# A transformer of four layers on one core: the second weight matrix loaded in two parts, and a new written order of instructions

## Chip, cores and metric

The kernel runs on one core of one Trainium2 chip. The metric is the device time of one execution in microseconds (us); of the kernel before nine runs are shown, and their median counts. TensorE (PE) multiplies matrices, with weight loads (PEld) that overlap the multiplications; ScalarE (ACT), VectorE (DVE) and GpSimd (POOL) work on tiles; SyncE (SP) issues most of the DMAs, ACT a few.

## What is computed

Four layers on 2048 tokens of 512 channels, 32 heads of 16 channels, everything handed over in bf16. Layers 1 and 3 are attention with a sliding window of 256 tokens (A), layers 2 and 4 linear attention over all tokens (B). Each pair uses the same weights twice.

```python
def _A_ref(x, wqkv, wo):
    B, S, D = x.shape
    H = 32; Dh = D // H; W = 256
    qkv = (lambda x, *d: x.transpose(*d))((x @ wqkv).reshape(B, S, 3, H, Dh), 2, 0, 3, 1, 4)
    q, k, v = qkv[0], qkv[1], qkv[2]
    scores = jnp.einsum("bhqd,bhkd->bhqk", q, k) * (Dh ** -0.5)
    idx = jnp.arange(S)
    mask = (idx[:, None] - idx[None, :] >= 0) & (idx[:, None] - idx[None, :] < W)
    scores = jnp.where(mask[None, None], scores, -1e9)
    p = _softmax(scores, axis=-1)
    o = jnp.einsum("bhqk,bhkd->bhqd", p, v)
    return (lambda x, *d: x.transpose(*d))(o, 0, 2, 1, 3).reshape(B, S, D) @ wo

def _B_ref(x, wqkv, wo):
    ...
    phi = lambda t: jnp.where(t > 0, t + 1, jnp.exp(t)) + 1e-6
    pq, pk = phi(q), phi(k)
    kv = jnp.einsum("bhsd,bhse->bhde", pk, v)
    z = jnp.einsum("bhsd->bhd", pk)
    num = jnp.einsum("bhqd,bhde->bhqe", pq, kv)
    den = jnp.einsum("bhqd,bhd->bhq", pq, z)[..., None] + 1e-6
    o = num / den
    return (lambda x, *d: x.transpose(*d))(o, 0, 2, 1, 3).reshape(B, S, D) @ wo

x = A_x
x = x + _A_ref(_layernorm(x, axis=-1), A_wqkv, A_wo)
x = x + _B_ref(_layernorm(x, axis=-1), B_wqkv, B_wo)
x = x + _A_ref(_layernorm(x, axis=-1), A_wqkv, A_wo)
x = x + _B_ref(_layernorm(x, axis=-1), B_wqkv, B_wo)
```

## The kernel before, in words

The tokens are 16 tiles of 128, in four chunks of 512. For a chunk of an A layer the kernel normalizes four tiles (`ln_tile`, `ln_sums`: statistics on DVE or ACT, the inverse root on POOL or ACT, the scaled tile `xn`), transposes each into `xnT` (`transpose`: on TensorE at L588 for chunks 0 and 1, by a DMA transpose from SP at L579 for chunks 2 and 3; each is about 1.25 us of issue on SP's queue), and projects queries and keys (`q_unit`, `k_unit`, each of which reads all four transposed tiles) and values (`v_unit`, one tile each). Every projection is one group of four matmuls of 512 columns at L569. Keys are written twice, masked for even and odd heads, into `kbd` (L779 on DVE, L777 on ACT); values go through `vst` and four DMAs per two tiles from SP into `vbd` (L798). `scores` makes groups of score matmuls (L822) into PSUM, one exponential on ACT (L840), masks on POOL (L873) or DVE (L868); `pv_group` multiplies with the values (L901) and divides (L915, L916) into `o_sb`. Its rows are transposed into `oT`, again by SP's DMA for chunks 0 to 2, and multiplied with `woA`; the sum goes into `xres` (`out_tile`, `out_rows`, L751, L755).

A B layer projects keys and values tile by tile and queries chunk by chunk with `wB` (`bk_unit`, `bv_unit`, `bq_units`), applies phi (`phi`: exponential L975 on ACT, a clamp L978 on DVE or POOL, a maximum L981 on DVE), sums keys times values (`kv_unit`, L1022), and at the end of the layer forms one matrix from the sums and `woB` (`kv_final`, L1059 to L1077), denominators (`norm_pair`, L1091 to L1104; `norm_unit`, L1117) and output rows (`p2_tile`). The chunks of B are worked off beside the attention of later chunks.

All of this is recorded first as operations of a `Planner`, numbered in the order in which they are recorded, with what each needs. `Planner.run` then emits them in the order of the long string `ORDER`: `646P` is operation 646 on TensorE, and A, V, G, S stand for ACT, DVE, POOL and SP; H marks a transfer's landing and emits nothing. Each engine's queue thus has its operations in the order of this string, and semaphores make them wait for what they need. The planner holds a model of time, with which the string was searched beforehand. At build time the model still decides one thing: where it sees a gap of over 0.45 us on TensorE, it puts filler matmuls on `identb` into a free PSUM bank (L491). In the model TensorE's clock is full in a window of 3.413 us if the window before it held at least 2750 columns (`is_warm`), and operations cost 1.28 to 2 times as much where it isn't.

The weights come in whole matrices. `wA` and the tokens are asked for at once, at the start, `wA` in five pieces; the last eight token tiles, `woA`, `wB` and `woB` are operations on ACT's queue (27, 29, 31 and 33), whose places are in `ORDER` too. A first time in the planner (15, 25, 40 and 70 us) keeps the search from putting them earlier. Operations 620, 624, 628 and 632 are the transposes of tiles 0 to 3 of chunk 2 in the first A layer, 646 is that chunk's third query projection, 636 its first.

Of the kernel before, what the change touches and what calls it, by code (L numbers as in the profile page):

```python
# [17 lines left out]
D = 512  # L18
# [132 lines left out]
class Planner:  # L151
# [25 lines left out]
    def run(self):  # L177
# [7 lines left out]
        def is_warm(t):  # L185
            k = int(t / self.WIN)
            for w in range(max(warm, default=-1) + 1, k + 1):
                warm[w] = mac.get(w - 1, 0) >= self.FULL
            return warm[k]
# [3 lines left out]
        for x in order:  # L193
            o, e = self.ops[int(x[:-1])], engine[x[-1]]
# [45 lines left out]
18H 17H 36V 6G 19H 20H 12A 41V 46V 37G 38V 51A 14A 23H 2G 42G 15A 13A 21H 3G 47G 10V 22H 24H 43V 39P 40V 25H 44P  # L240
52V 48V 45V 75P 76V 49P 53P 54V 77S 78P 50V 26H 65P 55P 79V 60P 62A 63P 16V 57V 56V 67A 0G 58P 80S 314V 59V 66V
64V 61A 27A 329V 73P 87P 88A 81P 4G 9G 1G 91P 84P 28H 82A 83S 5G 70P 315G 316V 319V 330G 324V 89G 96P 72V 71V
92A 7G 320G 101P 74A 85A 325G 95G 102A 321V 90G 68P 69V 317P 97A 107P 322P 86S 104G 94G 98G 106G 103G 108A 109G
115P 105G 99G 116A 331V 318V 354P 93G 332P 119P 323V 617V 618G 8G 100G 120A 110G 124P 117G 355V 326V 357P 125A
333V 629V 625V 621V 123G 129P 356S 327P 111P 112P 113P 128G 630G 130A 131G 358A 133V 328V 122V 135P 143P 114V
136A 121V 127G 619V 126G 134V 360P 144A 132G 147P 137G 118G 138G 631V 361V 359S 337P 620S 148A 916V 152P 139P
140P 153A 157P 928V 622G 141P 626G 158A 142V 149G 146G 160G 162G 155V 156G 363P 150G 161G 338A 364V 163P 171P
627V 623V 154V 164A 166G 165G 334P 347P 632S 362S 917G 159G 151G 175P 348V 172A 145V 336V 342P 343V 173G 920V
335V 180P 176A 185P 653P 181A 167P 168P 169P 174V 654V 186A 29A 921G 624S 628S 191P 199P 177G 183G 179V 918V
365S 192A 646P 170V 636P 647V 187V 190V 929G 184G 182G 203P 188G 189G 178V 200A 656P 208P 204A 194G 31A 213P  # L250
657V 193V 637V 201G 195P 641P 214A 196P 217V 206G 197P 209A 215V 930V 219P 227P 220A 642V 352P 216V 228A 198V
212G 211G 205G 218G 221G 924V 202G 207G 233P 210V 651P 652V 234A 366P 222G 232G 223P 224P 225P 371P 237V 655S
229G 230G 658S 235V 236G 238G 367A 372A 353V 231G 375P 376A 925G 239P 662P 373G 931S 379G 380P 226V 240V 659P
919S 374G 370G 663V 926V 381A 660V 369G 386P 339P 340V 341V 378V 387A 922V 377G 390P 391A 384V 344P 346V 398P
242S 345V 385G 633P 382G 635V 399A 248S 403P 349P 383G 251S 368G 389G 407P 245S 388G 393V 400V 634V 394P 392G
401V 923S 927S 404A 408A 402G 412P 395P 396P 418P 351V 413A 419A 416V 414V 935P 422P 423A 415V 405V 664S 417G
409G 410G 406V 350V 430P 397V 431A 936V 638P 421G 435P 436A 411V 420V 424V 643P 439P 426P 645V 440A 425G 444P
427P 445A 428P 450P 451A 644V 454P 639V 648P 446G 449G 437G 640V 438V 432V 452G 434V 455A 448G 661S 429V 433V
462P 940P 467P 453V 463A 443G 457G 468A 442G 447G 456V 932P 471P 941V 441G 458P 649V 241V 472A 459P 476P 477A
465G 460P 482P 650V 933V 934V 937P 483A 469V 464V 486P 243P 494P 487A 495A 474V 475V 461V 470V 244V 466G 479G  # L260
480G 945P 499P 500A 484V 481G 473V 488V 478G 489V 485G 490P 497V 939V 946V 938V 503P 504A 491P 508P 492P 514P
254V 505G 509A 510G 512G 493V 507G 515A 511V 249P 518P 519A 246P 32H 250V 516V 498G 526P 502G 527A 33A 517G 255G
247V 506G 513G 520G 532G 252P 521V 942P 536P 665P 501V 253V 496V 522P 530G 535G 523P 524P 944V 528G 537A 534G
533G 541V 540V 666A 531G 538G 529V 539V 670P 542P 674P 671A 675A 525V 543V 262V 551S 545S 548S 554S 952P 679P
680A 673V 685P 258V 943V 678V 953V 955P 672V 263G 677G 668G 686A 667G 256G 681V 956V 689P 688G 687G 690A 683G
684G 682G 257S 950P 669V 697P 698A 546P 702P 552P 692V 676V 547V 703A 706P 691G 693P 707A 711P 694P 557V 553V
565V 712A 699V 264G 695P 717P 270P 705G 259G 718A 951V 721P 729P 555P 271A 696V 549P 957S 722A 713G 558G 709V
720G 715V 704V 559V 266V 700V 730A 714G 710G 716G 719G 734P 735A 556V 701G 708G 723G 738P 724V 550V 569V 725P
743P 265S 954S 739A 260V 744A 731G 261S 267G 566G 726P 727P 749P 750A 732V 742G 958P 747G 570G 753P 754A 728V
272V 959V 544V 274P 761P 766P 762A 275V 741V 755V 746V 273V 767A 961P 571G 751V 756G 737G 745G 740G 733G 276P  # L270
770P 775P 962V 768V 752G 736G 284P 748V 757P 758P 759P 277A 776A 769V 771A 561V 278V 777V 781P 285A 780G 782A
279V 773V 760V 778V 785P 786A 560S 280P 793P 794A 764V 763G 774G 288P 798P 799A 572S 286V 287V 765G 562G 779G
567V 947P 802P 784G 772G 803A 783V 289V 789P 807P 563G 788G 787V 790P 808A 810G 949V 801V 805G 795V 568S 564S
948V 281V 791P 811G 804G 960S 813P 814A 815G 282P 605P 606A 268V 792V 797V 817P 818A 796V 806G 825P 601P 602A
283V 816V 826A 819G 812V 607V 963S 800G 613P 614A 809G 835P 608V 832G 827G 820G 833G 836A 603V 604V 609P 830V
831V 615V 964P 610A 965A 829G 828V 821P 822P 823P 969P 834V 616V 839G 840G 837G 838V 824V 841P 842V 970A 269S
290P 291A 973P 974A 978P 979A 844S 967G 971G 847S 850S 611V 981G 294P 612V 573P 295V 984P 985A 292V 293V 968V
966G 980G 845P 988P 989A 848P 982V 983G 996P 997A 846V 976V 972G 1001P 849V 991G 1002A 574A 853S 990G 975V 860V
986G 987G 977G 851P 852V 577P 1005P 1006A 992P 861G 1010P 1011A 864V 578V 856V 575V 576V 993P 994P 1016P 1017A
998G 296P 857G 1020P 995V 1015V 1021A 1012G 1013V 854P 1014V 1028P 1029A 297V 579P 580A 1033P 1034A 1008G 587P  # L280
1007G 1018G 1037P 1038A 1009G 1019V 11V 1004V 999G 1000G 1003G 1023V 855V 1022V 1031V 858G 1024P 1025P 1026P
1042P 1043A 1048P 1049A 1044G 1030G 865G 581V 582V 1027V 868V 1039G 862G 583P 1052P 588A 1053A 1041V 584V 591P
1060P 1061A 592V 593P 585P 859S 1032G 35S 589V 590V 586V 1065P 1066A 863S 1035V 1046V 1040V 1047G 594A 1045G
1050G 1055V 597P 876P 1069P 1070A 598V 1036G 843V 1051G 1074P 1075A 1056P 1064G 1054G 866G 1057P 877V 1077G
1068V 867S 1058P 1067G 1080P 1081A 595V 1072V 882P 596V 1084P 1085A 599P 1079V 883V 1092P 1063G 1073G 1059V 872P
1076V 600V 1078G 890P 1093A 1071G 1097P 891V 873A 1098A 298P 299A 1101P 1102A 874V 1106P 878P 1082G 875V 1107A
1083V 1062V 869G 1087G 1086V 300V 1095V 1088P 1089P 879A 1090P 1112P 1113A 870G 871S 1110G 1100G 1104G 1099V
1116P 1117A 301V 886P 1091V 1105G 880V 1111G 1103G 302P 881V 1096V 884P 1109G 1108V 1115V 887A 303A 1124P 1134P
1114G 1094G 885V 1119G 1118G 888V 304V 889V 305V 1120P 1121P 1122P 1135A 1123V 1125A 34H 1133V 1132V 1131V 892P
1139G 1136G 893A 894V 1129V 1138G 895V 896P 1137G 1128G 1127G 306P 1126G 897A 1130G 1140P 898P 1141V 1143P 899V  # L290
1142V 307A 1144A 1151P 308G 1152V 1147P 1148A 1155P 1145P 1149P 309V 900P 1153P 1146V 1156A 1157P 1150V 1237V
1159A 1160A 1161G 1164V 1154V 1165A 310P 901A 1158V 1169A 1162P 1163V 1174A 1238P 1239V 904P 902V 1166G 1170G
311A 1167P 903V 1179P 312V 1171G 313V 1175G 1183P 1168A 905A 1172P 1189P 906V 1173A 1176G 907V 1185P 1193P 1180A
1184A 1186A 1181V 1190V 1182V 1177P 1178V 1194A 1187V 1188V 1195G 1197P 908P 1207P 1198V 1196V 1208A 1191P 1199P
1200A 1203P 1209V 1192V 1210V 1201V 1202V 909A 1215P 1204A 1216A 1217V 1218V 1211P 1205P 1206V 1223V 912P 913A
1225V 1219P 1240P 1241P 1224G 910V 1220A 1212A 914V 915V 1242A 1226G 911V 1213V 1227P 1214V 1243A 1221G 1228A
1222V 1244V 1851P 1538P 1539V 1233P 1536P 1235P 1537V 1234A 1231P 1236A 1247P 1248V 1232A 1229P 1852P 30H 1245P
1230A 1540P 1246V 1853A 1541V 1546P 1249P 1250V 1854A 1251P 1252V 1253P 1254V 1544P 1548A 1545V 1855V 1255P
1542P 1549G 1257A 1258G 1262A 1259G 1267A 1263A 1256V 1547V 1264G 1260P 1268A 1261A 1543V 1856P 1272A 1265P
# [76 lines left out]
def build(ctx, tc, A_x, A_wqkv, A_wo, B_x, B_wqkv, B_wo, out, force_safe=False):  # L376
    nc = tc.nc
# [94 lines left out]
    def fast_network(ctx_f):  # L472
# [52 lines left out]
        def B(*key):  # L525
            return bufs.setdefault(key, Buf())
# [459 lines left out]
        def bk_unit(key, i):  # L986
            X, u = xT[key], i % 4
            ks = slot("pks")
            t = {}
# [452 lines left out]
```

## Time and profile before

| | |
|---|---|
| median of 9 runs | 463.15 us (458.75 to 466.12) |
| profiled execution | 464.8 us, of which the span from first to last instruction is 463.1 us |
| busy | PE 94%, DVE 80%, ACT 82%, POOL 56% of the span |
| mean granted TensorE clock | 0.989 of full |
| ACT's exponentials (L840) | 246, 284.2 us |
| projections (L569) | some 960 matmuls, 63.7 us the largest of six groups |
| scores (L822), values (L901) | 94.0 and 83.7 us on TensorE |
| DMAs from SP into vbd (L798) | 128, 1.9 us to landing (median) |
| DMA transposes into xnT, oT (L579) | 40 and 24, 2.5 us to landing (median) |
| woA, wB, woB | 512, 1536 and 512 KB, 5.3, 7.5 and 3.7 us to landing |

A row of a group names the line, the engine, the operation, the tile written and the tiles read, then how often, the busy time and the mean of one in ns, then the engine's idle time ahead of these instructions and what ended it. A line can be that of a helper: every projection is at L569, whatever it computes. The clock row is in tenths of full speed over 40 equal slices, and 9 is 90% or more. Matmuls overlap, so that a group's mean (380 ns at 512 columns) is longer than the distance from one to the next.

### The profile page before, as it was taken

What the parts mean: (1) busy time and instruction counts of PE and PEld (TensorE: products, weight loads), DVE (VectorE), ACT (ScalarE), POOL (GpSimd) and SP (SyncE); (2) the same over time, 40 slices, a digit from 0 to 9 for tenths busy, and PEclk for the clock granted to TensorE, in tenths of its full rate; (3) what the DMA queues carried; (4) which work ended last, traced back from release to release, by engine and by line L of the source; (5) the groups of instructions that cost most, each with busy time, mean ns of one, the idle gap of its engine ahead of it and who ended that gap; (6) DMA issues with size and microseconds to landing.
All of it is one profiled execution on the core that took longest, in us unless ns stands there. A gap on an engine that the chain in (4) does not pass through costs nothing.

```text
span 463.1 us, 15167 instructions
## 1 busy us (share of the span) xinstructions
PE 436.5 (94%) x6035; PEld 227.7 (49%) x6103; DVE 368.4 (80%) x969; ACT 379.0 (82%) x442; POOL 258.8 (56%) x737
## 2 busy tenths in 40 slices
PE   7997999999999999999999998999999989999893
PEld 3454554555555556543445454465455545564331
DVE  5896677878887987878877888888887777776983
ACT  7798599989999999656888888989999989967630
POOL 5297344367755585432324577865685548465431
PEclk8999899999999999999999999999999999999998
DMA  7425631023222010000021124111322123000014
GB/s 226 122 47 120 179 72 26 3 70 71 38 51 58 13 25 15 2 1 0 5 45 27 27 47 72 40 34 26 70 56 42 24 26 37 14 2 1 1 54 135
DMA packets 53806, 22.29 MB, mean 48 GB/s; under 512 B 38368, under 2 KB 53216, under 8 KB 53728
## 3 DMA queue, kind: packets, MB, share of 16 engines
q1 hardware_dynamic: 49760, 16.80, 17.2%
q10 hardware_dynamic: 3968, 4.46, 3.0%
q8 instruction: 49, 0.80, 0.7%
q14 instruction: 29, 0.24, 0.2%
HBM read 6.29 MB, written 2.10 MB: 18 GB/s over the span
## 4 chain that ended last, share of the span: by engine, by line
PE 74%; DVE 8%; ACT 6%; issue 5%; DMA 2%; POOL 1%; SPq 0%; ACTq 0%; DVEq 0%; POOLq 0%
PE psb L569 40%; PE psb L901 15%; PE psb L822 13%; ACT pt L840 6%; PE psb L1117 2%; PE psb L588 2%; POOL pt L873 1%; DMA wA<-in_A_wqkv_dram 1%; DVE kbd L779 1%; DMA oT<-o_sb 1%; PE psb L491 1%; DVE pqT L981 1%; PE psb L1091 1%; DVE ln_st L690 1%; DVE zc L1059 1%
## 5 line engine op out<-in xcount | busy, mean ns | idle before, releaser
L840 ACT ACTIVATE pt<-psb 128x1536 bf16<-128x1536 f32 (+2 forms) x246 | 284.2, 1215 | 31.2 <-PE psb L822 20.1
L873 POOL TENSOR_SCALAR_AFFINE_SELECT pt<-pt 128x192 bf16<-128x192 bf16 (+2 forms) x535 | 157.4, 328 | 113.1 <-ACT pt L840 109.0
L822 PE MATMUL psb<-qT,kbd 32*128 32x320 bf16 (+4 forms) x1440 | 94.0, 254 | 3.9 <-ACT pt L840 2.7
L901 PEld LDWEIGHTS <-pt 128*128 128x128 bf16 x2880 | 78.0, 96 | 13.6 <-issue 9.7
L901 PE MATMUL psb<-vbd,pt 128*128 128x34 bf16 x2880 | 83.7, 178 | 0.2 <-DVE xres L755 0.2
L868 DVE TENSOR_TENSOR pt<-pt,tri 128x128 bf16<-128x128 bf16 (+4 forms) x262 | 64.6, 279 | 11.4 <-ACT pt L840 11.0
L822 PEld LDWEIGHTS <-kbd 32*128 32x128 bf16 x1440 | 40.2, 92 | 66.1 <-issue 59.7
L569 PE MATMUL psb<-xnT,wA 128*128 128x512 bf16 x241 | 63.7, 386 | 3.7 <-issue 3.0
L569 PE MATMUL psb<-wB,xnT 128*128 128x512 bf16 x235 | 61.6, 380 | 1.6 <-DVE pqT L978 0.4
L569 PEld LDWEIGHTS <-xnT 128*128 128x128 bf16 x384 | 32.6, 98 | 41.9 <-issue 12.4
L779 DVE TENSOR_TENSOR kbd<-psb,eo 128x512 bf16<-128x512 f32 x58 | 37.9, 680 | 2.9 <-PE psb L569 2.6
L569 PEld LDWEIGHTS <-wA 128*128 128x128 bf16 x256 | 21.8, 99 | 30.4 <-issue 10.8
L569 PE MATMUL psb<-wA,xnT 128*128 128x512 bf16 x116 | 33.7, 396 | 2.0 <-DMA wA<-in_A_wqkv_dram 1.2
L569 PE MATMUL psb<-woA,oT 128*128 128x512 bf16 x120 | 31.5, 381 | 3.3 <-DMA oT<-o_sb 2.6
L569 PE MATMUL psb<-xnT,wB 128*128 128x512 bf16 x121 | 31.5, 380 | 0.9 <-DVE vflags L968 0.5
L569 PE MATMUL psb<-wkv,pqT 128*128 128x512 bf16 x123 | 29.6, 380 | 0.3
L690 DVE BATCH_NORM_STATS2 ln_st<-xres 128x6 f32<-128x512 f32 (+1 forms) x39 | 26.5, 680 | 2.0 <-DMA xres<-in_A_x_dram 1.9
L916 DVE TENSOR_TENSOR o_sb<-psb,rall 128x384 bf16<-128x384 f32 (+1 forms) x48 | 24.6, 513 | 1.7
L975 ACT ACTIVATE pqT<-psb 128x512 bf16<-128x512 f32 x32 | 18.9, 599 | 8.2 <-PE psb L569 6.4
L556 DVE CAST qT<-psb 128x512 bf16<-128x512 f32 x29 | 19.8, 685 | 6.7 <-PE psb L569 6.0
L624 POOL TENSOR_TENSOR ln_rs<-ln_rs,mhalf 128x1 f32<-128x1 f32 x39 | 21.9, 561 | 3.3
L981 DVE SCALAR_TENSOR_TENSOR pqT<-psb,pqT 128x512 bf16<-128x512 f32 x32 | 21.8, 687 | 1.6 <-POOL pqT L978 1.0
(122 smaller groups left out, 486.2 us busy)
## 6 DMA issues: line engine op xcount, KB each, us to landing
vbd<-vst SPq DMA_DIRECT2D x128, 34.0 KB, 1.9
out_dram<-ost SPq DMA_DIRECT2D x16, 128.0 KB, 1.8
wB<-in_B_wqkv_dram ACTq DMA_DIRECT2D x1, 1536.0 KB, 7.5
xres<-in_A_x_dram ACTq DMA_DIRECT2D x1, 1024.0 KB, 5.5
xnT<-xn SPq DMA_TRANSPOSE x40, 2.5
wA<-in_A_wqkv_dram SPq DMA_DIRECT2D x1, 512.0 KB, 6.6
xres<-in_A_x_dram SPq DMA_DIRECT2D x1, 512.0 KB, 7.3
woA<-in_A_wo_dram ACTq DMA_DIRECT2D x1, 512.0 KB, 5.3
```

The lines of the kernel that those rows point to most:

```text
L556: (nc.scalar.copy if e == "ACT" else nc.vector.tensor_copy)(dst(), src())
L569: nc.tensor.matmul(t["t"][:], lhsT=lhs(c), rhs=rhs(c), start=(c == 0), stop=(c == NCT - 1))
L624: nc.gpsimd.tensor_tensor(out, out, mhalf[:, 0:1], op=ALU.pow)
L690: nc.vector.bn_stats(t["st"][:], x())
L779: nc.vector.tensor_tensor(kbd[r][:, t, :, :, :].rearrange("p m k h -> p (m k) h"), ps()[:, hf * 256:(hf + 1) * 256].unsqueeze(2).to_broadc ...
L822: nc.tensor.matmul(A[:, x, at[x]:at[x] + w, :], lhsT=kbd[half(m)][32 * rg:32 * rg + 32, tt, m % 4, :, :], rhs=qT[I % 2][32 * rg:32 * rg + ...
L840: nc.scalar.activation(body[:, x:y, 0:pos[x], :], t["A"][:, x:y, 0:pos[x], :], ACT.Exp, scale=0.25)
L868: nc.vector.tensor_tensor(v, v, mt, op=ALU.mult)
L873: nc.gpsimd.affine_select(out=v, in_=v, compare_op=ALU.is_ge, fill=0.0, base=1 if kind == 0 else -2, pattern=[[0, n], [2 * sg, 64]], chann ...
L901: nc.tensor.matmul(t["O"][:, u, g, :, :], lhsT=PT[:, s0:s0 + 2, :], rhs=vbd[half(m)][:, m % 4, :, grp[g], :], start=(n == 0), stop=(n == l ...
L916: nc.vector.tensor_tensor(o_sb[:, u0:u0 + nu, h0 * DH:(h0 + 2 * ng) * DH].rearrange("p u (h e) -> p u h e", e=DH), Ov[:, :, :, 0:DH], r.to ...
L981: nc.vector.scalar_tensor_tensor(out=dst(), in0=ps()[:], scalar=1.0 + 1e-6, in1=dst(), op0=ALU.add, op1=ALU.max)
```

## The change

`wB` gets two landings in place of one, `B("wB", 1)` for the columns of keys and values and `B("wB", 0)` for those of queries, each loaded by a DMA of its own from ACT's queue, of 1 MB and 512 KB. The readers name the part they need. The first times become 19 us for `woA`, 22 and 27 us for the parts of `wB`; the assumed landings of the pieces of `wA` and of tiles 4 to 7 become 0.5 to 1.5 us later. In the model TensorE's clock is full from 25 us on. The string `ORDER` is a new one throughout, with other places and in part other engines for the same operations; on POOL, DVE and ACT some masks, evacuations and clamps trade engines, and there are 41 filler matmuls in place of 37. As one load has become two, every operation from 33 on has a number higher by two: 646 is now 648, and 620, 624, 628 and 632 are 622, 626, 630 and 634. The new operations 31 and 33 are the parts of `wB`, 35 is `woB`; 29 is still `woA`. Of the string the lines around `woA` and the first part of `wB` are shown.

```diff
--- before.py
+++ after.py
@@ -183,6 +183,8 @@
         mac, warm, mode = {}, {}, ""
 
         def is_warm(t):
+            if t > 25.0:
+                return True
             k = int(t / self.WIN)
             for w in range(max(warm, default=-1) + 1, k + 1):
                 warm[w] = mac.get(w - 1, 0) >= self.FULL
@@ -237,138 +239,138 @@
...
-136A 121V 127G 619V 126G 134V 360P 144A 132G 147P 137G 118G 138G 631V 361V 359S 337P 620S 148A 916V 152P 139P
...
-627V 623V 154V 164A 166G 165G 334P 347P 632S 362S 917G 159G 151G 175P 348V 172A 145V 336V 342P 343V 173G 920V
-335V 180P 176A 185P 653P 181A 167P 168P 169P 174V 654V 186A 29A 921G 624S 628S 191P 199P 177G 183G 179V 918V
-365S 192A 646P 170V 636P 647V 187V 190V 929G 184G 182G 203P 188G 189G 178V 200A 656P 208P 204A 194G 31A 213P
...
+365P 629V 624G 143P 160A 165P 155A 173P 153G 151G 919G 632G 147G 340V 926V 625V 622S 344P 163G 157G 166A 366V
+152V 144V 162G 364S 177P 164V 161G 174A 345V 633V 349P 350V 178A 655P 656V 167V 158G 148G 156G 182P 187P 626S
+31A 188A 336P 169P 175G 183A 930V 337V 168G 170P 191V 179V 630S 927G 171P 172V 193P 634S 192G 367S 180G 201P
+194A 181G 648P 638P 205P 176G 195V 202A 185G 931G 190G 649V 338V 206A 29A 658P 920V 184V 196V 210P 659V 922V
...
@@ -990,7 +992,7 @@
             def pre():
                 t["t"] = bw.tile([P, D], BF, name="pks", tag=f"pk{ks.k}", bufs=1)
             o, s, ps = proj(lambda c: X["t"][:, c, u * P:(u + 1) * P], lambda c: wB[:, c, D:2 * D],
-                            reads=[B("wB"), B("xq", i)], deps=lastk, use=X["slot"], take=[ks], pre=pre)
+                            reads=[B("wB", 1), B("xq", i)], deps=lastk, use=X["slot"], take=[ks], pre=pre)
             lastk[:] = [o]
             f = phi(lambda: t["t"][:], ps, s, o, use=[ks])
             kv_in[i] = [(t, ks, f)]
@@ -1002,7 +1004,7 @@
             def pre():
                 t["t"] = vss[vs_.k]
             o, s, ps = proj(lambda c: X["t"][:, c, u * P:(u + 1) * P], lambda c: wB[:, c, 2 * D:3 * D],
-                            reads=[B("wB"), B("xq", i)], deps=lastv, use=X["slot"], take=[vs_], pre=pre)
+                            reads=[B("wB", 1), B("xq", i)], deps=lastv, use=X["slot"], take=[vs_], pre=pre)
             lastv[:] = [o]
             def fe(e):
                 (nc.scalar.copy if e == "ACT" else nc.vector.tensor_copy)(t["t"][:, :, 0:32], ps()[:].rearrange("p (j c) -> p j c", c=32))
@@ -1035,7 +1037,7 @@
             if not INPLACE:
                 for t in range(NCT):
                     o, s, ps = proj(lambda c, t=t: wB[:, c, t * P:(t + 1) * P], lambda c: X["t"][:, c, :],
-                                    reads=[B("wB")] + [B("xq", 4 * I + u) for u in range(4)], use=X["slot"], frees=[B("pq", I, t)])
+                                    reads=[B("wB", 0)] + [B("xq", 4 * I + u) for u in range(4)], use=X["slot"], frees=[B("pq", I, t)])
                     phi(lambda t=t: pqT[:, t, I * 512:(I + 1) * 512], ps, s, o, writes=[B("pq", I, t)])
                 return
             w, wide[0] = wide[0], True
@@ -1043,7 +1045,7 @@
             before = [d for u in range(4) for d in B("xq", 4 * I + u).r]
             for t in range(NCT):
                 ps.append(proj(lambda c, t=t: wB[:, c, t * P:(t + 1) * P], lambda c: X["t"][:, c, :],
-                               reads=[B("wB")] + [B("xq", 4 * I + u) for u in range(4)], deps=lastq + before))
+                               reads=[B("wB", 0)] + [B("xq", 4 * I + u) for u in range(4)], deps=lastq + before))
                 lastq[:] = [ps[t][0]]
             wide[0] = w
             read = [d for u in range(4) for d in B("xq", 4 * I + u).r]
@@ -1129,12 +1131,13 @@
         NI = NSS
         b_x = [B("x", i) for i in range(NT)]
         landed = [([b_x[i]], 3.65) for i in range(4)]
-        landed += [([B("wA", 1, 0)], 5.5), ([B("wA", 0, 0)], 5.5), ([B("wA", 2)], 8.0), ([B("wA", 1, 1)], 10.0), ([B("wA", 0, 1)], 9.5), (b_x[4:8], 12.0)]
+        landed += [([B("wA", 1, 0)], 5.5), ([B("wA", 0, 0)], 5.5), ([B("wA", 2)], 9.5), ([B("wA", 1, 1)], 11.0), ([B("wA", 0, 1)], 10.5), (b_x[4:8], 12.5)]
         for b, t in landed:
             pl.op({"HBM": .01}, lambda e: None, writes=b, after=t)
         for b, t, c, fn in ((b_x[8:NT], 15.0, 3.0, lambda e: load_x(nc.scalar, 8, NT - 8)),
-                            ([B("woA")], 25.0, 1.5, lambda e: nc.scalar.dma_start(woA[:], wcols(A_wo, 0))),
-                            ([B("wB")], 40.0, 4.5, lambda e: nc.scalar.dma_start(wB[:], wcols(B_wqkv, 0, 3))),
+                            ([B("woA")], 19.0, 1.5, lambda e: nc.scalar.dma_start(woA[:], wcols(A_wo, 0))),
+                            ([B("wB", 1)], 22.0, 3.0, lambda e: nc.scalar.dma_start(wB[:, :, D:3 * D], wcols(B_wqkv, 1, 2))),
+                            ([B("wB", 0)], 27.0, 1.5, lambda e: nc.scalar.dma_start(wB[:, :, 0:D], wcols(B_wqkv, 0))),
                             ([B("woB")], 70.0, 1.5, lambda e: nc.scalar.dma_start(woB[:], wcols(B_wo, 0)))):
             o = pl.op({"ACT": .5}, fn, after=t)
             pl.op({"HBM": c + 2.0}, lambda e: None, deps=[o], writes=b)
```

## Prediction

> **What bounds the kernel now.** I read the page first: busy shares and the granted clock.
>
> ```profile
> PE 436.5 (94%) x6035; PEld 227.7 (49%) x6103; DVE 368.4 (80%) x969; ACT 379.0 (82%) x442; POOL 258.8 (56%) x737
> ...
> PEclk8999899999999999999999999999999999999998
> ```
>
> TensorE is busy for 436.5 of 463.1 us, so all its idle time is 26.6 us, and an order that adds or removes no matmul can win only from that, from the half-clock stretches and from the joints between matmuls. The clock row dips only at the start and in the fifth slice. So I cut the stretch around the fifth slice into steps of 4 us (per engine busy us and instructions, then clock, DMA share, GB/s).
>
> ```profile
> 36.00:40.00 4.00, 4.00 (x37) 1.59 (x37) 3.36 (x9) 3.65 (x5) 3.64 (x12) 1.00 0.34 75
> 40.00:44.00 4.00, 3.21 (x78) 2.21 (x71) 3.07 (x8) 3.13 (x4) 2.62 (x9) 1.00 0.81 195
> 44.00:48.00 4.00, 1.87 (x5) 0.78 (x7) 1.76 (x4) 1.38 (x2) 2.11 (x8) 0.83 0.28 68
> 48.00:52.00 4.00, 4.00 (x44) 1.58 (x43) 1.64 (x7) 1.48 (x2) 0.29 (x1) 0.74 0.24 42
> ```
>
> TensorE loses 2.92 us there and then runs below full clock. The timeline of that stretch says what it waited for:
>
> ```profile
> 38.59 2.52 SPq L579 DMA_TRANSPOSE xnT<-xn  x2
> ...
> 40.51 0.41 ACTq L1136 DMA_DIRECT2D woA<-in_A_wo_dram  x1
> ...
> 46.07 3.02 PE L569 MATMUL psb<-xnT,wA 128*128 128x512 bf16 x7 [2.86 <-issue]
> 46.08 0.42 DVE L701 TENSOR_SCALAR xn<-xres,ln_mv,ln_rs 128x512 bf16<-128x512 bf16 x1 [2.98 <-DMA xnT<-xn]
> ```
>
> PE's wait carries the label "issue", but VectorE comes free at the same moment, and its releaser is the DMA transpose into xnT. The DMA view of 41.1 to 42.2, in which only the later transpose counts, gives its time to landing:
>
> ```profile
> xnT<-xn SPq DMA_TRANSPOSE x1, 6.1
> ```
>
> The median of all 40 on the page is 2.5 us. It was issued at about 39.9 and landed at 46.0; woA (512 KB, issued at 40.51, 5.3 us) landed at 45.8. In the written order before these are 624S, 628S (transposes), 29A (woA) and 646P, the third query projection of tokens 1024 to 1535, which reads all four transposes. The waits of TensorE on DMA elsewhere are small:
>
> ```profile
> PE psb L569 <- DMA oT<-o_sb: 2.6, 2, 1.3
> ```
>
> **What the Trainium skill says.** "DMA: Bandwidth & Descriptors", "Queues, rings and completion order": each DMA engine takes turns between the queues it has work for, a packet at a time. So a transpose on SP's queue shares with a weight load on ACT's. The trace agrees: 6.1 against 2.5 us. "TensorE: Matmul & The Clock Gate", "What's actually happening": idleness puts TensorE at half clock, activity for about 3.4 us brings it back. The trace agrees: seven 512-column matmuls after the stall take 3.02 us, 0.43 each. Same page, "Back-to-back issue gap": 512/2.4 + 2.5 = 216 ns; a run of 24 takes 5.20 us in the chain of waits, 217 each.
>
> **The change, part by part.** The profiled execution took 464.8 us, its span 463.1, so 1.7 lie outside; the median of nine runs is 463.15, 1.65 lower. I sum on 464.8 and subtract 1.65 at the end.
>
> (1) *Loading wB in two parts.* One more DMA issue on ACT's queue (0.4 us, issued ahead of running work). It removes no wait: wB landed at 49.7 + 7.5 = 57.2, and TensorE first reads it at 109.99; in the order that is TensorE's 165th step before and its 170th after. Cost by itself 0. What counts is where the loads stand.
>
> (2) *Loads against transposes.* After, the 1 MB part (31A) stands directly behind 626S and ahead of 630S and 634S, the last two transposes that 648P (646P of before, again TensorE's 60th step) needs; one PE step, 201P, lies between 634S and 648P, two between 628S and 646P before. I place 31A in time by ACT's queue. Before, from the first exponential (18.85) to woA stand 8 of 1.45, 11 of 0.92 and 5 copies of 0.62 us: 24.8. After, to 31A, 7, 10 and 4: 21.8. Three us less work, of which 1.7 go to a later first exponential (4 fills of vbd at 2.0 us now all stand behind the statistics) and idle: I take 39.2, an estimate, 1.3 before woA. woA cost the transpose 6.1 - 2.5 = 3.6 us. Twice the bytes ahead cost at most 7.2, less the 1.3 us head start: 5.9, 2.3 more than before; if shares, not bytes, decide, 0. I take +1.2, and 0.3 for a longer stretch at half clock: **+1.5** (from -4.8, stall and clock loss gone, to +4). The clock loss of before is 3.02 - 7 x 0.217 = 1.5, plus 0.26 and 0.19 on the next two groups, 1.9; with 2.86 it makes 4.8.
> woA then stands where wB stood (49.7), a third of its bytes; TensorE was 3.95 of 4 us busy beside wB, so nothing is won: 0. The 512 KB part of wB (33A) and woB (35A) follow TensorE's 96th and 107th steps, just behind 929S and 925S, read by the 105th. Nine steps of 436.5/714 = 0.61 us are 5.5 us of cover; two transposes need 1.25 issue + 2.5, and 3.6 more beside a load: 7.35. Between 0 and 1.85: **+0.7**.
>
> (3) *All other transposes.* I count TensorE steps between a transpose and the projection that reads it. A landing of 2.5 us is four steps. Without the trio above the shortfall below four is 23 steps before and 35 after (readers zero or one step behind: two before, eight after; three of them, 1466S, 1472S and 1873S, at TensorE's steps 420 to 445). Since the 23 cost 2.6 us of measured DMA wait, 0.11 each, 35 cost 4.0: **+1.4**. Bounds: 0, as a transpose starts when its data and SP's queue allow, not where the list has it; and 12 x 0.61 = 7.3 if nothing runs ahead.
>
> (4) *Joints.* The instruction lists have 195 separate runs of scores before and 183 after. A projection of four matmuls between scores takes 1.04 us, against 4 x 0.217 = 0.87 in a long run. Part of that overlaps the scores: the chain counts 0.97. 12 x 0.10 = **-1.2** (0 to -2.0).
>
> (5) *Nothing or near it.* Filler matmuls on identb rise from 37 to 41, placed where the planner sees gaps: 4 x 0.217 if a gap is not there, 0.9 at most; taken 0, since idle TensorE covers them. ACT sheds 4 half evacuations of keys (0.55 each) and two squares (0.91), and gains two rstd pairs (0.58): about -3 us of 379; VectorE gains 15 masks of 192 (0.28) and sheds 12 of 128 and 256: about +2 of 368; GpSimd about +4 of 259, with two more clamps at 1.94 in place of VectorE's 0.32. TensorE covers all of it while it is at 98% in the attention stages; -1 to +2 if the clamps hold a bank. Taken 0.
>
> Sum: 0 + 1.5 + 0.7 + 1.4 - 1.2 = +2.4: 467.2 profiled, 465.55 as a median: **465.6**.
>
> **Rivals.** *The stall goes (faster).* 31A starts 1.3 us before woA; if 634S also goes out earlier than its place in the list, both land before TensorE reaches 648P at about 43.2. Then -4.8 - 1.2, with the later terms at half (+1.0): -5.0, 458.2. For it: 18.9 us are busy in 20 to 40, SP's queue has four transposes and four vbd issues either way. Against: a load of 1 MB took 5.5 us alone, and 39.2 + 5.5 is 44.7. It decides from the point where the stall is under 0.9 us.
> *Nothing moves (same).* The split has no reader to serve, the stall stays 2.86, the written places of transposes don't bind, and joints and fills cancel: -1.2 + 0.7 + 0.5 = 0, 463.2. For it: TensorE's work is the same matmuls at the same clock. Against: eight tight readers instead of two.
> The forecast's upper end: 630S and 634S are served only after the load. 39.2 + 7.5 = 46.7, and 2.6 behind it: 49.3, a stall of 6.1 and half clock for longer, +5; with (3) at +3 that makes +8: 471.
>
> **How the numbers follow.** Measurement can tell about 0.5% (2.3 us) from no change. Forecast, slower by over that, 0.40, its own range 465.5 to 472; nothing moves, 0.33; stall gone, 0.27. To leave 2 in 10 out the range reaches from just below the faster case, 457.5, to 472.
>
> **What would show it.** Right on (2): a TensorE gap of 3 us or more ahead of the same query projection near 43 to 48 us, with the xnT transpose landing in 6 us or more beside wB, and the clock row dipping in the same slice. Right on (3): waits of L569 (line moved by two) on DMA oT or xnT above 2.6 us. Right on (4): TensorE's busy time near 435. Right on (1): no wait on wB in either. I am wrong if the clock row is full in slices four and five, or if the gap moves to where no transfer is under way.

## The result, and the profile after

The kernel after takes 469.94 us in the median of ten runs (466.85 to 471.34), the kernel before 462.95 in the runs beside it: ratio 1.015, 95% interval 1.012 to 1.018. The change makes the kernel slower, by 7.0 us. The profiled spans are 463.1 and 469.9 us. Lines of after are those of before plus 2, from L1136 on plus 3.

Busy shares and the clock row of after, to be set beside the two lines of before:

```profile
PE 439.1 (93%) x6044; PEld 228.7 (49%) x6107; DVE 367.3 (78%) x975; ACT 377.6 (80%) x437; POOL 263.1 (56%) x739
...
PEclk9989797799999999999999999999999999999998
```

Before, the clock row had one dip after the start, in the fifth slice. Now it has four, in the third, fifth, seventh and eighth slices, all in the first 95 us. TensorE's waits in after say what stands there (line waited for, releaser, total, times, longest):

```profile
PE psb L824 <- ACT pt L842: 7.5, 14, 4.1
PE psb L571 <- DMA xnT<-xn: 4.0, 2, 3.6
PE psb L493 <- ACT vst L558: 1.5, 1, 1.5
...
PE psb L571 <- DMA oT<-o_sb: 0.8, 1, 0.8
```

Three long waits: 4.1 us on an exponential, 3.6 on a transpose, 1.5 on a copy of values. The wait on oT, 2.6 us before, is down to 0.8. The steps of 4 us of after show where each lies (columns as in the table of before: TensorE's busy time comes second, then weight loads, DVE, ACT, POOL, and clock, DMA share, GB/s at the end):

```profile
20.00:24.00 4.00, 2.11 (x13) 0.88 (x13) 2.66 (x7) 2.83 (x4) 1.66 (x6) 0.83 0.19 43
...
44.00:48.00 4.00, 0.38 (x9) 0.14 (x2) 0.86 (x3) 2.26 (x2) 2.29 (x8) 0.82 1.24 137
48.00:52.00 4.00, 3.78 (x12) 1.17 (x12) 2.01 (x5) 0.00 (x0) 0.00 (x0) 0.50 0.11 26
...
72.00:76.00 4.00, 2.35 (x19) 1.04 (x19) 2.86 (x8) 0.00 (x0) 2.14 (x8) 1.00 0.57 76
76.00:80.00 4.00, 1.51 (x12) 0.72 (x12) 0.36 (x2) 3.02 (x3) 0.97 (x3) 0.66 0.60 170
80.00:84.00 4.00, 4.00 (x24) 1.02 (x22) 2.48 (x4) 1.79 (x3) 0.00 (x0) 0.50 0.10 26
```

At a clock of 0.50, as from 80 to 84, TensorE is busy but slow: four matmuls of 512 columns take 1.89 us there (at 81.39), against 1.04 at full clock (at 37.35). I call the three stalls by their order.

**First stall, near 20 us.** The timeline of after from 14 to 23:

```profile
14.33 0.38 ACTq L407 DMA_DIRECT2D xres<-in_A_x_dram  x1
...
21.17 0.59 ACT L558 CAST vst<-psb 128x512 bf16<-128x512 f32 x1 [2.01 <-DMA vbd<-vst]
...
21.81 0.81 PE L493 MATMUL psb<-identb 128*128 128x512 bf16 x3 [1.55 <-ACT vst L558]
```

The load of the last eight token tiles (27A, 1 MB) starts 1.2 us earlier than before. The copy of values waits until a transfer into vbd has released its buffer, and TensorE waits for that copy.

**Second stall, at 44 us: the one forecast.** The timeline of after from 37 to 50, then its DMA view of 41.1 to 42.2, the same window as before:

```profile
38.16 3.93 SPq L581 DMA_TRANSPOSE xnT<-xn  x3
...
39.18 0.38 ACTq L1139 DMA_DIRECT2D wB<-in_B_wqkv_dram  x1
...
47.87 0.59 PE L571 MATMUL psb<-xnT,wA 128*128 128x512 bf16 x1 [3.62 <-DMA xnT<-xn]
```
```profile
xnT<-xn SPq DMA_TRANSPOSE x1, 6.9
```

31A is issued at 39.18 (forecast: 39.2), the last transpose takes 6.9 us in place of 6.1, the stall is 3.62 us in place of 2.86.

**Third stall, at 74 us: a place forecast, but not this mechanism.** The timeline of after from 70 to 80:

```profile
69.61 2.37 ACT L842 ACTIVATE pt<-psb 128x1536 bf16<-128x1536 f32 x2 [0.26 <-PE psb L824]
...
74.65 5.26 SPq L800 DMA_DIRECT2D vbd<-vst  x8
76.47 0.39 ACTq L1140 DMA_DIRECT2D wB<-in_B_wqkv_dram  x1
76.98 3.71 ACT L842 ACTIVATE pt<-psb 128x1536 bf16<-128x1536 f32 x3 [5.01 <-DMA vbd<-vst]
78.49 0.61 PE L824 MATMUL psb<-qT,kbd 32*128 32x320 bf16 x9 [4.08 <-ACT pt L842]
```

ACT ends an exponential at 71.98 and then does nothing for 5.01 us, and what releases it is no matmul but a transfer into vbd. What is next in its queue is 33A, the issue of wB's 512 KB part. The reason stands in the built program, the instruction lists that are made from the kernel: the DMAs of SP and ACT take eight completion semaphores (counters that a DMA raises when it has landed) in turn. 33A is the 74th, so it takes the semaphore of the 66th, and the program makes its issue wait until that one has landed: the first of the vbd transfers issued at 74.65, which takes 1.8 us to landing: 76.45. The exponentials behind 33A wait with it, though they need neither transfer.

An anchor for the rest: the small matmul on `ones_bf` (L965, L967 after) first runs at 195.6 us before and at 205.3 after. At the end after is 6.8 us late. So the first part lost 9.7 us and the remainder won 2.9 (463.1 - 195.6 = 267.5 against 469.9 - 205.3 = 264.6 us).

### The profile page after: what moved, and what is told of

It reads as the page before. It is cut to its first block, busy times and chain, and to the rows that moved or that the text cites. A ratio compares the mean times of both kernels' runs of the same rounds, so it can differ in the third digit from the quotient of the medians.

```text
span 469.9 us, 15197 instructions
## 1 busy us (share of the span) xinstructions
PE 439.1 (93%) x6044; PEld 228.7 (49%) x6107; DVE 367.3 (78%) x975; ACT 377.6 (80%) x437; POOL 263.1 (56%) x739
## 4 chain that ended last, share of the span: by engine, by line
PE 75%; ACT 7%; DMA 6%; DVE 6%; issue 3%; ACTq 0%; SPq 0%; DVEq 0%
PE psb L571 41%; PE psb L903 14%; PE psb L824 14%; ACT pt L842 5%; DMA xnT<-xn 2%; DMA oT<-o_sb 2%; PE psb L1119 2%; PE psb L590 2%; DMA vbd<-vst 1%; ACT vbd L552 1%; PE psb L493 1%; DVE pqT L983 1%; DMA xres<-in_A_x_dram 1%; DVE pt L870 1%; PE psb L1093 1%
## 5 line engine op out<-in xcount | busy, mean ns | idle before, releaser
L875 POOL TENSOR_SCALAR_AFFINE_SELECT pt<-pt 128x192 bf16<-128x192 bf16 (+2 forms) x532 | 154.2, 323 | 116.0 <-ACT pt L842 115.1
L870 DVE TENSOR_TENSOR pt<-pt,tri 128x192 bf16<-128x192 bf16 (+4 forms) x268 | 65.4, 276 | 19.2 <-ACT pt L842 18.6
L571 PE MATMUL psb<-xnT,wA 128*128 128x512 bf16 x240 | 65.8, 399 | 5.0 <-DMA xnT<-xn 3.6
L917 DVE RECIPROCAL rall<-psb 128x24 f32<-128x24 f32 (+1 forms) x48 | 13.8, 288 | 18.6 <-PE psb L903 17.0
L983 DVE SCALAR_TENSOR_TENSOR pks<-psb,pks 128x512 bf16<-128x512 f32 x32 | 21.8, 684 | 3.5 <-POOL pks L980 3.0
```

Source lines behind the costliest of these rows:

```text
L571: nc.tensor.matmul(t["t"][:], lhsT=lhs(c), rhs=rhs(c), start=(c == 0), stop=(c == NCT - 1))
L870: nc.vector.tensor_tensor(v, v, mt, op=ALU.mult)
L875: nc.gpsimd.affine_select(out=v, in_=v, compare_op=ALU.is_ge, fill=0.0, base=1 if kind == 0 else -2, pattern=[[0, n], [2 * sg, 64]], chann ...
L983: nc.vector.scalar_tensor_tensor(out=dst(), in0=ps()[:], scalar=1.0 + 1e-6, in1=dst(), op0=ALU.add, op1=ALU.max)
```

## The experiments

All moved-load kernels have the string `ORDER`, the planner's model and the filler matmuls of the kernel they start from. Only the emission of a load's DMA on ACT's queue moves, behind another operation of ACT:

```diff
             o.fn(e)
+            for f in self.also.get(o.n, ()):
+                f(e)
...
-            o = pl.op({"ACT": .5}, fn, after=t)
+            to = MOVED.get(len(pl.ops))
+            o = pl.op({"ACT": .5}, fn if to is None else lambda e: None, after=t)
+            if to is not None:
+                pl.also.setdefault(to, []).append(fn)
```

Lines there are those of the kernel they start from plus 5. Kernel 5 is the kernel of experiment 5, and so on. Times are medians, ratios are to the kernel before in the runs beside it, with 95% intervals. Differences to after are differences of medians. Before itself was at 462.95 us beside after and at 463.2 to 464.3 beside the experiments, so that the same differences taken from the ratios are another number: 6.4 in place of 5.8 in experiment 1, 7.1 in place of 6.4 in experiment 2, and up to 1.6 us apart in the others. Read them as good to 1 or 1.5 us.

**1 and 2. One pair of loads moved.** First woA and wB's 1 MB part, then wB's 512 KB part and woB.

```diff
+MOVED = {31: 206, 29: 230}
```

> The changed kernel, all else equal, with the two loads that met the transposes of chunk 2 moved on ACT's queue: the 1 MB part of wB behind the third query projection of that chunk, woA five exponentials behind it. Theory (three places early in the kernel, at 20, 44 and 72 us, where a load meets SP's small transfers, cost the time, each by an idle TensorE and half clock after it): the stall of 3.6 us before that projection shrinks below 1 us and the clock stays full from 44 to 56 us, 5 to 6 us less than the changed kernel, about 464.5. Rival (the new written order gives transposes too little cover, whoever loads beside them): the stall stays within 1 us of 3.6, the time within 2 us of 470.

464.15 us, ratio 1.001 (0.998 to 1.005): 5.8 us below after, as expected.

```diff
+MOVED = {33: 502, 35: 511}
```

> The changed kernel with only the 512 KB part of wB and woB moved later on ACT's queue, by 49 and 43 operations of ACT or fewer, to about 100 us. Theory: the gap of TensorE at 74 to 78 us (4.1 us, ACT idle 5.0) goes, with the half clock to 87 us: 5 to 7 us less than the changed kernel, about 464. Rival (the gap comes from the new order of exponentials and scores): it stays, time within 2 us of 470.

463.5 us, ratio 1.000 (0.998 to 1.002): 6.4 us below after, as expected. The waits of the two kernels, first and second in this order, show that each move takes away one stall and leaves the other:

```profile
PE psb L829 <- ACT pt L847: 7.5, 14, 4.1
...
PE psb L576 <- DMA xnT<-xn: 1.0, 2, 0.6
```
```profile
PE psb L576 <- DMA xnT<-xn: 4.2, 2, 3.7
PE psb L829 <- ACT pt L847: 3.4, 13, 0.5
```

So 5.8 us are the price of the second stall and 6.4 us that of the third, idle time and half-clock stretch together.

**3 and 4. The token load later; all three moves.**

```diff
+MOVED = {27: 84}
```

> The changed kernel with only the 1 MB load of tokens 1024 to 2047 moved behind ACT's third copy into vst. Theory: ACT's wait of 2.0 us for the DMAs of vbd at 19 us goes, TensorE's gap of 1.55 us at 20 us and the half clock from 20 to 28 us with it: 3 to 4.5 us less than the changed kernel, about 466. Rival (the start is bound by the projections, and the gap is made up for by slack before the first attention): within 1 us of 470.

472.17 us, ratio 1.018 (1.011 to 1.024): a miss, no gain. The wait on the copy of values is gone, but a new one stands at 22 to 26 us, because the statistics of those tokens now wait 4.08 us for the load to land. From the waits of this kernel:

```profile
PE psb L595 <- DVE xnT L598: 3.2, 1, 3.2
```

```diff
+MOVED = {31: 206, 29: 230, 33: 502, 35: 511, 27: 84}
```

> The changed kernel with the three moves at once. Theory: the sum of the three, 13 to 16 us less, about 455 to 457, below the kernel before, because the new order is faster where no load is under way (its second half took 2.9 us less than that of before). Rival (the three gaps share one slack, so that the second and third recover what the first lost): 463 to 466.

460.6 us, ratio 0.992 (0.990 to 0.994): 9.3 us less than after, where 13 to 16 were expected. 2.7 us of that new wait are still in it.

**5. Both pairs moved, the token load in its place.**

```diff
+MOVED = {31: 206, 29: 230, 33: 502, 35: 511}
```

> The kernel after, with only the two pairs of loads moved (31A and 29A behind the third query projection, 33A and 35A behind 502A and 511A); the token load stays in its place. Theory (the two stalls are separate and both come from where the weight loads stand): the single moves gained 5.8 and 6.4 us against the kernel after, so together 469.9 - 12.2 = 457.7 us, ratio to before 0.988; and less than the kernel with all three moves (460.6), since the token move cost 2 us by itself. Both dips of the clock row between 40 and 90 us gone. Rival (the moves gain only what the order loses elsewhere, or a new stall opens once both are gone, as the token move opened one): 461 or more, and a wait of TensorE of 2 us or more in the first 100 us in a new place.

458.24 us, ratio 0.989 (0.986 to 0.993): the two gains add up (5.8 + 6.4 = 12.2 expected, 11.7 measured), and no new wait of 2 us or more opens. The clock row of this kernel shows no dip any more, and the first two of its waits show that the third stall is gone and 2.1 us of the first are left:

```profile
PEclk9999999999999999999999999999999999999997
```
```profile
PE psb L829 <- ACT pt L847: 3.4, 13, 0.5
PE psb L498 <- ACT vst L563: 2.1, 1, 2.1
```

**6. The third stall: queue or bytes?** The 512 KB part of wB and woB from GpSimd's queue, at the same places.

```diff
-([B("wB", 0)], 27.0, 1.5, lambda e: nc.scalar.dma_start(wB[:, :, 0:D], wcols(B_wqkv, 0))),
-([B("woB")], 70.0, 1.5, lambda e: nc.scalar.dma_start(woB[:], wcols(B_wo, 0)))):
+([B("wB", 0)], 27.0, 1.5, lambda e: nc.gpsimd.dma_start(wB[:, :, 0:D], wcols(B_wqkv, 0))),
+([B("woB")], 70.0, 1.5, lambda e: nc.gpsimd.dma_start(woB[:], wcols(B_wo, 0)))):
```

> The kernel after, with 33A (the 512 KB part of wB) and 35A (woB) issued from GpSimd's queue at the same places in the list; same bytes, same places. Theory (ACT's queue stands behind a load whose issue waits, and the exponentials queue behind it): ACT runs on, TensorE's 4 us wait on the exponentials near 72 to 78 us is gone, about 464 us as with the loads moved later, ratio to before 1.00; GpSimd's queue stands instead, and it has slack. Rival (the load itself, by its bytes beside the transposes and the block-diagonal V transfers, makes the exponentials late): the transfer is the same, the wait stays at about 4 us, 469 to 471 us, ratio 1.015.

466.14 us, ratio 1.008 (1.004 to 1.012): between the two, 3.8 of the 6.4 us (by the ratios 3.3 of 7.1). The timeline from 70 to 86:

```profile
71.96 1.00 POOL L1145 DMA_DIRECT2D wB<-in_B_wqkv_dram  x1
...
72.71 4.71 ACT L847 ACTIVATE pt<-psb 128x1536 bf16<-128x1536 f32 x4 [0.51 <-PE psb L829]
...
77.92 1.04 PE L576 MATMUL psb<-xnT,wA 128*128 128x512 bf16 x4 [1.66 <-DMA xnT<-xn]
```

In the built program GpSimd's DMAs have eight semaphores of their own, and this load, the first of them, has no wait before its issue. It goes out at 71.96, ACT runs on, and the 4.1 us wait on the exponentials is gone. The load is now 4.5 us earlier and runs beside the transposes issued from 70 us on, and TensorE waits 1.66 us for one of those: what my prediction had put here. So the blocked queue is shown to make the wait on the exponentials, and taking it away wins about half of the third stall's price. That the bytes cost the rest is read from the wait of 1.66 us and not shown by a run of its own. The run takes away ACT's wait and the wait of the issue itself together, and doesn't tell these two apart. It also gives the DMAs of SP behind the load other predecessors, as two are gone from their count.

**7. The stall of before, taken away in before.**

```diff
+MOVED = {29: 200, 31: 228}
```

> The kernel before, with only its woA and wB loads (29A, 31A) moved behind the third query projection of tokens 1024 to 1535. Theory (the stall of 2.9 us near 43 us in the kernel before is the same thing as the one of 3.6 us in the kernel after: a transpose that shares the transfer engines with a weight load): the wait falls under 1 us, the dip of the clock row in its fifth slice goes, 463.0 - 4.8 = 458.2 us, ratio 0.990. Then the new order without load stalls is worth nothing or little against the old one. Rival (the old stall is the transposes' own lateness, and the load has little to do with it): the wait stays over 2 us, 462 to 464 us.

462.0 us, ratio 0.998 (0.996 to 1.000). A miss in size. The old stall is shorter and its clock dip is gone (wait at 44 us 1.25 us), but wB, now issued at 51.75, meets other transposes: the two issued from 52.94 on take 6.3 us to landing, 3.9 in before. Timeline of this kernel from 44 to 64:

```profile
61.00 0.47 DVE L706 TENSOR_SCALAR xn<-xres,ln_mv,ln_rs 128x512 bf16<-128x512 bf16 x1 [2.08 <-DMA xnT<-xn]
...
62.12 1.02 PE L574 MATMUL psb<-xnT,wA 128*128 128x512 bf16 x4 [1.32 <-DVE vst L561]
```

In this order the move was worth 1.2 us, hardly clear of noise, and not the 4.8 that the old stall's idle time and half clock add up to. The new waits, of which 1.32 us show here, are one reason; whether they are the whole reason isn't shown.

**8. The split alone, in the order of before.** The 1 MB part where wB stood, the 512 KB part right behind it; readers name their part as in the change, and `ORDER` has the old order with the numbers from 33 on one load higher.

```diff
-([B("wB")], 40.0, 4.5, lambda e: nc.scalar.dma_start(wB[:], wcols(B_wqkv, 0, 3))),
+([B("wB", 1)], 40.0, 3.0, lambda e: nc.scalar.dma_start(wB[:, :, D:3 * D], wcols(B_wqkv, 1, 2))),
+([B("wB", 0)], 40.0, 1.5, lambda e: nc.scalar.dma_start(wB[:, :, 0:D], wcols(B_wqkv, 0))),
```

> The kernel before in its own order, with wB loaded in two parts in the same place: the 1 MB part where wB stood, the 512 KB part right behind it. One part of the change alone. My prediction priced this at nothing: 463 us, ratio 1.000, since TensorE reads wB 50 us later. Rival (one more load shifts which earlier transfer each later issue has to wait for, and the second part stands in ACT's queue until such a transfer has landed, with exponentials behind it): TensorE waits on ACT's exponentials for 2 us or more near 50 us, 465 us or more.

463.72 us, ratio 1.000 (0.996 to 1.004). Both issues follow each other without a gap, at 49.43 and 49.85: the transfer whose semaphore the second takes had landed. The split itself costs nothing here; in after it is the place of its second part that costs.

**9. The second stall: how much is the size of the load?** woA and wB's 1 MB part in each other's places.

```diff
+MOVED = {31: 29, 29: 31}
```

> The kernel after, with 29A (woA, 512 KB) and 31A (the 1 MB part of wB) in each other's places, so that half the bytes stand ahead of the transposes 630S and 634S. My prediction priced the doubled bytes at 1.2 us of its 1.5. Theory (bytes ahead of the transpose decide): the wait of 3.6 us falls to 1 to 2.9 us and the time by 1 to 2.5 us, to 467.4 to 469, ratio to before 1.010 to 1.013. Rival (any load there makes the transposes late, and TensorE's half-clock stretch is as long): the wait stays at 3.4 us or more and the time at 469 to 471, ratio 1.015.

466.96 us, ratio 1.006 (1.003 to 1.008): 3.0 us below after by the medians and 4.3 by the ratios, more than expected. The wait falls from 3.62 to 1.81 us. The last two transposes, under issue between 39.5 and 40.8, land, by the DMA views of that window of this kernel and of after:

```profile
xnT<-xn SPq DMA_TRANSPOSE x2, 5.0
```
```profile
xnT<-xn SPq DMA_TRANSPOSE x2, 7.3
```

Against 2.5 us as the median of the page, half the bytes ahead cost about half the delay (2.5 against 4.8). Not all of the gain need come from that: the second stall shrinks by 1.8 us of idle time and 1.7 of clock, but the clock loss behind the other two stalls is smaller in this profile as well (0 and 1.7 us in place of 1.7 and 5.1), with waits as long as in after.

**10 to 12. The first stall.** Both pairs moved, and the token load later by less than in 3, then earlier, in two places.

```diff
+MOVED = {31: 206, 29: 230, 33: 502, 35: 511, 27: 64}
```

> The kernel with both load pairs moved (458.2 us), and the load of tokens 1024 to 2047 (27A) moved as well, but only behind the second half evacuation of keys (64A), some 1.5 us later than in the kernel after. With the move by 3 us the wait on the value copies (2.1 us) went and one on the statistics (3.2 us) came. Theory (there is a place between the two, as in the kernel before, which issued this load 1.2 us later and had no stall at 20 us): neither wait over 1.2 us, about 457 us, ratio 0.987. Rival (the two waits overlap in their causes: what the transfers of V win, the statistics lose): 2 us or more of wait in sum near 20 to 26 us, 458 to 460 us.

459.69 us, ratio 0.990 (0.986 to 0.993), the same as without this move, so a miss: the wait on the copy of values is 1.9 us still.

```diff
+MOVED = {31: 206, 29: 230, 33: 502, 35: 511, 27: 14}
```

> The kernel with both load pairs moved, and the load of tokens 1024 to 2047 (27A) issued some 4 us earlier, behind the second filling of vbd (14A, near 10.3 us). Theory (the first stall near 20 us is one more case of a load beside transfers: the V transfers issued between 15 and 18 us take 5.2 to 5.8 us to land in place of 1.9, because this load of 1 MB runs from 14.8 to 21.3): the load has landed by about 17, those transfers land in 2 to 3 us, TensorE's wait of 2.1 us on the value copy falls under 1, and no wait on the statistics takes its place; 456 to 457 us, ratio 0.985. Rival (the earlier load delays the first V transfers or the second part of the first weights instead, and TensorE waits between 8 and 16 us): 458 to 461.

455.64 us, ratio 0.982 (0.977 to 0.988).

```diff
+MOVED = {31: 206, 29: 230, 33: 502, 35: 511, 27: 81}
```

> As the kernel before it in this call, with the token load 2 us earlier instead of 4, behind the first value copy (81A, near 12.7 us). Theory (its 6 us then end near 19): a part of the gain, the V transfers issued from 17 us on land in 2 to 3 us and the wait on the value copy is near 1 us, 457 us, ratio 0.987. Rival (it meets the first V transfers and gains nothing): 458 to 461.

455.46 us, ratio 0.982 (0.977 to 0.988), where 457 was expected. Both have four runs. The load is issued at 6.47 us in the first of these two, earlier than I had meant, and at 11.39 in the second, against 14.78 in kernel 5. The transfers into vbd under issue between 15 and 16.5 us, by the DMA views of kernel 5 and of the kernel with the load at 6.47:

```profile
vbd<-vst SPq DMA_DIRECT2D x3, 34.0 KB, 5.8
```
```profile
vbd<-vst SPq DMA_DIRECT2D x3, 34.0 KB, 1.9
```

With that the wait on the copy of values is out of the list, and TensorE is 3.99 of 4 us busy from 20 to 24. So the first stall is the same thing as the second: 1 MB beside small transfers that something waits for. The way out is earlier, because the tokens are needed too. These two are the fastest versions of the study, 14.5 us below after and 8 below the kernel before beside them, with every matmul in the order of after.

**The clock model** was not run by itself: with the model of before and the `ORDER` of after all five engines get the same operations in the same order as in after; only two groups of matmuls near the end swap their PSUM banks. Taking the clock as full acts through the searched order.

**The order without its stalls.** Kernel 5 and kernel 7 are the two orders with the least stall of loads and the same mean clock, 0.994. Their traces have as many matmul records as weight loads, so that none is missing (those of before and after lack some 60, and their busy times can't be compared this closely). The busy line and the row of the scores from the page of kernel 7 (old order), then of kernel 5 (new order):

```profile
PE 439.1 (95%) x6103; PEld 227.4 (49%) x6103; DVE 368.4 (80%) x969; ACT 378.9 (82%) x442; POOL 258.6 (56%) x737
...
L827 PE MATMUL psb<-qT,kbd 32*128 32x320 bf16 (+4 forms) x1440 | 93.7, 253 | 3.7 <-ACT pt L845 2.6
```
```profile
PE 435.7 (95%) x6107; PEld 226.7 (50%) x6107; DVE 367.6 (80%) x975; ACT 377.6 (83%) x437; POOL 262.6 (57%) x739
...
L829 PE MATMUL psb<-qT,kbd 32*128 32x320 bf16 (+4 forms) x1440 | 92.2, 253 | 3.9 <-ACT pt L847 3.4
```

The new order has four more matmuls and 3.4 us less busy time, 1.5 of it in the scores, and takes 458.24 against 462.0 us beside the same runs of before. By these two kernels it is the better one in itself, though neither is free of load stalls (2.1 us are left in kernel 5, 1.25 and 1.3 in kernel 7).

## Why the prediction came out as it did

The forecast's direction and range held: 465.6 us, from 457.5 to 472, against 469.94. Its sum was +2.4 us, the change is +7.0. The range was wide, and took in the cases of no change and of a faster kernel too; the direction came out right although the largest cost was one that the sum didn't have, and a cost that it had, (3), isn't seen. So part of it is luck. By its steps:

- **(1) The split by itself, 0: right.** Experiment 8 gives a ratio of 1.000.
- **(2) 31A ahead of the transposes, +1.5: right in mechanism and place, too small.** Issue at 39.18, stall 3.62 against 2.86. With the clock loss of the slices that is 7.0 us after and 4.6 before, +2.4; by what the removals brought, 5.8 and 1.2, it is +4.6. The upper case (a stall of 6.1) did not come. The term for the doubled bytes, +1.2, was too low for this order: half the bytes gave back 3.0 to 4.3 us, of which the half-clock stretch is a part.
- **(2) 33A and 35A, +0.7 with an upper bound of 1.85: the step that failed.** It was sized as a transfer beside two transposes. Moving the pair away brought 6.4 us, and the 4.1 us stall there has another cause: 33A stands on ACT's queue and waits for an unrelated transfer, with the exponentials behind it. Taking it off that queue alone brought 3.8. I asked what is queued behind SP's transposes, and not what is queued behind the load itself, which I took for an issue of 0.4 us "ahead of running work". In before woB is the 74th DMA and has the same kind of wait, but stands later (issued at 94.61), where its transfer has long landed; so the page of before shows no such wait, and only the numbering of the DMAs in the built program would have.
- **(3) Other transposes with less cover, +1.4: not seen.** From the anchor on TensorE waits 2.6 us on DMA before, and 0.8 on oT and 0.4 on xnT after. That it is less isn't shown: in the profiles of the two other kernels in the old order the waits from there on are 1.3 and 1.4 us, in the eleven in the new order 1.1 to 2.3. The written distance between a transpose and its reader was no measure of the wait; the lower bound, 0, was nearer.
- **(4) Joints, -1.2 (to -2.0): right in sign, too small.** Between kernels 7 and 5 the scores alone give -1.5, all groups -3.4. The sign that I had named, a busy time near 435 us, shows in kernel 5 (435.7) but not in after (439.1), where half-clock stretches lengthen the matmuls. Taking joints between scores only left out those of transposes on TensorE (`xn`: 9.6 against 8.6 us) and of other projections.
- **(5) Fills and the start, 0: wrong for the start.** I gave no price to the place of the token load. It is issued 1.2 us earlier, and the first stall is worth 2.8 us (experiment 5 against the last). Fillers cost 1.0 us more of busy time (11.7 and 12.7).

With measured terms, the second stall is +2.4 or +4.6 (see above), the third +6.4, the first +2.8, waits on DMA from the anchor on 1.2 - 2.6 = -1.4 and busy time -3.4: +6.8 or +9.0, against 7.0 measured. This does not close the account. Each term is good to 1 or 1.5 us, -1.4 is within what such waits differ by between profiles, and the sum leaves out the very start, where before runs below full clock and after doesn't. The lines of before:

```profile
8.00:12.00 4.00, 3.18 (x15) 1.72 (x15) 2.60 (x6) 4.00 (x4) 1.27 (x5) 0.64 0.67 232
12.00:16.00 4.00, 3.95 (x18) 1.78 (x18) 2.80 (x4) 2.42 (x3) 0.00 (x0) 0.93 0.23 52
```

That is 1.7 us of clock. Two of three profiles of the old order have such a dip there, none of the eleven of the new one. Why, and how the old second stall is to be counted, stays open.

Of the rivals, "the stall goes" fell: it asked for a stall under 0.9 us. "Nothing moves" fell as well, by 7 us. The faster time of the first rival, 458.2, is what kernel 5 reaches, where the loads no longer stand before waiting work; its sum was another, so the equal number is chance.

## What to carry to other kernels

Of a load that is moved, ask three things: which small transfers with a waiting reader run in its 5 to 7 us, what the issuing engine has queued behind it, and which earlier DMA its completion semaphore has to wait for. Splitting a load was free here, but in the built program it adds one to the count of DMAs and so gives every later one another predecessor. The size of a stall in a trace is not what its removal brings (1.2 of 4.8 us in experiment 7, where the moved load met other transposes); a gain counts when the kernel without the stall has been timed.

## What was not expected of the hardware

- A DMA issue on ACT's queue held ACT for 4.5 us (71.98 to 76.47) until an unrelated transfer of 34 KB, issued by SP, had landed, as the built program asks; the same load from GpSimd's queue, with no such wait in the program, went out at once, and ACT ran on.
- Small transfers suffer more than the loads that they meet: 34 KB into vbd takes 5.8 us in place of 1.9, two transposes 7.3 (median) in place of 2.5, about in proportion to the bytes ahead (5.0 with half of them), while the load of 1 MB takes 6.1 against 5.1 us in its quieter place (experiment 9).
- The three stalls of 1.5, 3.6 and 4.1 us cost 1.7, 3.4 and 5.1 us of clock in the profile of after (one less the granted clock, times 4, summed over the slices; a part of it falls into the idle time itself), but not in every execution: after the first stall the slice of 20 to 24 us shows a clock of 0.83 in the profile of after and 1.00 in that of experiment 5, with a longer wait (2.1 against 1.5 us), and behind the third stall, 4.1 us long in both, the profile of experiment 9 loses 1.7 us of clock in place of 5.1. What decides this was not tried.
